# An attention stage in front of dense experts: squares without their scaling, sums of two operands, copies on ScalarE, an earlier weight load

## The chip, the cores and the metric

The kernel runs on one core of a Trainium2 chip. The metric is the device time of one execution in microseconds, the median of several runs. All arithmetic is fp32 (matmul operands are split into a high and a low part of a shorter form, so that three matmuls make one precise product).

## The reference

Three stages follow one another. The first is attention by random features over q, k, v of shape (2, 8, 576, 64) with 128 features:

```python
q_s, k_s = q * scale, k * scale               # scale = 64 ** -0.25
def phi(x):
    proj = x @ omega.T
    h = proj - sum(x * x) / 2                 # sum over the 64 of a head
    return exp(h - max(h)) / sqrt(128)
kv = phi(k_s).T @ v ; z = sum(phi(k_s))       # per batch and head
out = phi(q_s) @ kv / (phi(q_s) @ z + 1e-6)
```

Its output, seen as 1152 tokens of 512, goes through four experts (`relu(x @ w1[e]) @ w2[e]`, weighted by `p[:, e]` and summed) and then through `h = x @ w_in; (h * cos(h)) @ w_out`.

## The kernel before

Every engine's instructions are issued in an order written out by hand, in one program; engines run their own lists in order and wait for one another by semaphores. Attention is a loop of steps `s` over eight pairs of a batch and two heads, and a ninth for the 64 tokens of each head that are left over. Step `s` makes the features of q of pair `s` and of k of pair `s + 1`, finishes `kv` of pair `s - 1` and the numerators, and writes the output of pair `s - 2` into the token tile `x` (`put_x`: transposes `tx` on TensorE, high part `xh` on ScalarE, low part `xl` on VectorE). What comes ahead of step 0 (k and q of pair 0, k of pair 1, the left-over tokens of k) is written out in line.

The parts that the change touches:

- `norms_ahead` squares a tile of q or k on POOL and halves it by additions, 512 to 256 to 128 elements per partition, then scales it by `-SC * SC / 2` (line 1024). `features` reduces what is left on VectorE to one number per row (`three[:, :, 1]`, line 1074), takes the maxima of the projections `pj` from PSUM (`three[:, :, 0]`, line 1080), and makes of both the shift `nb` by two reductions over pairs of neighbours (lines 1089 and 1092). ScalarE's exponentials (`phk`, `phq`, line 1099) read `nb`. POOL's tiles of q and k are loaded by SP, two buffers each; a load waits until POOL and TensorE have read the buffer's old content.
- `k_features(s + 1, s < first)` puts off k's shift while `s` is under 6: it comes in the next step, behind VectorE's copy of `xT` (`turn_ahead`: q and k transposed, half copied by VectorE at line 1303, half by ScalarE at line 1301).
- `kv_of` copies the finished `kv` from PSUM on VectorE (line 1168).
- `load_a(0, p, "p")` and `load_v2` bring the first expert's weights: SP loads a piece `ra_0p`, `ra_1p`, ... into one of two `raw` buffers, ScalarE writes its high part (`w02h`, line 129), POOL the low part (`w02l`, `w1l`, ..., line 134). These are generators; `advance(wload)` moves each one on by one stage, twice in a step, and `fetched` says at the end of which step each begins. Piece 0 is loaded at the end of step 2, its high half made in the middle of step 4, its low half at the end of step 4.
- `dense` is the stream of the experts' matmuls. From step 6 on, some of them are placed in each attention step (`plain`, line 549, four quanta of six matmuls), and the first second-layer products (`g`, line 779) follow. Those read `sth` (ScalarE) and `stl` (VectorE, line 752).
- `token_sums` makes the sums of token columns (T1 to T4) that the first expert's blocks need, on VectorE and ScalarE, one stage per quantum of the stream. `less` (lines 300 to 303) makes two full-width subtractions.

Of the kernel before, what the change touches and what calls it, by code (L numbers as in the profile page):

```python
# [12 lines left out]
ACTF = mybir.ActivationFunctionType  # L13
ALU = mybir.AluOpType
AX = mybir.AxisListType
# [11 lines left out]
def performer_moe_kernel(ctx, tc, q, k, v, omega, probs, w1, w2, w_in, w_out, out):  # L27
    nc = tc.nc
# [16 lines left out]
    SC = float(D) ** -0.25  # L45
# [72 lines left out]
    LEAD = 5  # L118

    def wait(n):  # L120
        for _ in range(n):
            yield
# [31 lines left out]
    def load_a(e, p, what="as"):  # L154
        aside = (e, p) == (0, NPF - 1) and what == "as"
        if aside:
            raw = late["h"][:, :, p, :KD, :].rearrange("p i k f -> p i (k f)")
            r4 = late["h"][:, :, p, :KD, :]
        else:
            raw = new_raw(f"ra{e}_{p}{what}")  # L160
            r4 = raw.rearrange("p (i k f) -> p i k f", i=2, k=KD)
        if e < E:
            for i in range(2):
                f0 = (i * NPF + p) * P
                nc.sync.dma_start(
                    out=r4[:, i], in_=w1[e, :, f0 : f0 + P].rearrange("(k p) f -> p k f", p=P)
                )
        else:
            nc.sync.dma_start(out=raw, in_=kept["a", e, p][0])
        def shaped(parts):  # L170
            return [x.rearrange("p (i w) -> p i w", i=2) for x in parts] if aside else parts

        eng = nc.gpsimd if e == 0 and what != "as" else nc.vector
        yield from wait((3 if p < 3 else 2) if what == "p" else LEAD)
        if what != "s":
            kind = "p" if what == "p" else "a"
            yield from place(kind, e, p)
            parts = split(eng, raw, *shaped(units[kind, e, p]))
            next(parts)
            if (what, p) != ("p", 2):  # L180
                yield
            yield from parts
            loaded.add((kind, e, p))
        if what == "p":
            if p < 2:
                units["a", e, p] = units["p", e, p]
                holder[f"w{2 * p}"] = ("a", e, p)
                loaded.add(("a", e, p))
            return
        a11, a12, a21, a22 = (r4[:, i, 2 * j : 2 * j + 2] for i in range(2) for j in range(2))  # L190

        def op(dst, x, y, o):
            eng.tensor_tensor(out=dst, in0=x, in1=y, op=o)

        op(a22, a21, a22, ALU.add)
        op(a21, a11, a21, ALU.subtract)
        yield
        op(a11, a22, a11, ALU.subtract)
        op(a12, a12, a11, ALU.subtract)
        yield from wait(2 if e < E else int(e > E or p != 2))  # L200
        yield from place("s", e, p)
        more = split(eng, raw, *shaped(units["s", e, p]))
        next(more)
        yield
        yield from more
        loaded.add(("s", e, p))
# [92 lines left out]
    def less(r, n, ks, cols):  # L299
        h, l = (x.bitcast(F32) for x in tokens(n, ks, cols))  # L300
        minus(r, h, r)
        nc.vector.tensor_tensor(out=r, in0=r, in1=l, op=ALU.add)
# [35 lines left out]
    def token_sums(cols):  # L338

        r1, r2 = spare(cols)  # L340
        whole(r2, tokens(0, LO, cols))
        whole(r1, tokens(1, LO, cols))
        if not cols.start:
            yield
        minus(r1, r1, r2)
        yield
        parts = sum_out(1, r1, cols)
        next(parts)
        yield
        yield from parts  # L350
        less(r1, 1, HI, cols)
        yield
        yield from rest_sums(r1, r2, cols)
# [596 lines left out]
    with tc.tile_pool(name="at1", bufs=1) as at1, tc.tile_pool(name="at2", bufs=2) as at2:  # L950
# [63 lines left out]
        def norms_ahead(nm, t):  # L1014

            x2 = at2.tile([P, 2 * R, D], F32, tag=f"x2{nm[0]}", name=f"x2_{nm}")
            nc.gpsimd.tensor_tensor(out=x2, in0=t, in1=t, op=ALU.mult)
            w = D
            while w > 16:
                w //= 2  # L1020
                nc.gpsimd.tensor_tensor(
                    out=x2[:, :, 0:w], in0=x2[:, :, 0:w], in1=x2[:, :, w : 2 * w], op=ALU.add
                )
            nc.gpsimd.tensor_scalar(
                out=x2[:, :, 0:w], in0=x2[:, :, 0:w], scalar1=-SC * SC / 2, scalar2=None, op0=ALU.mult
            )
            sqs[nm] = x2[:, :, 0:w]

        def turn(nm, t, pieces=1):
# [28 lines left out]
        def features(nm, turned, phi, squares=None, shift_later=False):  # L1058

            nb = at2.tile([P, 2 * R], F32, tag=f"nb{nm}"[:3], name=f"nb_{nm}")  # L1060
            pjs = [bank(f"pj_{nm}_{g}") for g in range(2)]
            for i in range(R):
                c = slice(i * P, (i + 1) * P)
                for z, (x_, y) in enumerate([(turned, ws)] + [(squares, minus_norm)] * (squares is not None)):
                    for g, pj in enumerate(pjs):
                        r = slice(g * D, (g + 1) * D)
                        nc.tensor.matmul(
                            pj[:, i * M : (i + 1) * M], x_[r, c], y[r, :],
                            start=z == 0, stop=z == (squares is not None),
                        )  # L1070
            yield
            three = at2.tile([P, 2 * R, 3], F32, tag=f"th{nm[0]}", name=f"three_{nm}")
            def square_sum():
                nc.vector.tensor_reduce(out=three[:, :, 1], in_=sqs.pop(nm), op=ALU.add, axis=AX.X)

            if squares is None and nm != "q0":
                square_sum()
            for g, pj in enumerate(pjs):
                to = (nb if squares is not None else three[:, :, 0])[:, g : 2 * R : 2]
                nc.vector.tensor_reduce(  # L1080
                    out=to, in_=pj.rearrange("p (a m) -> p a m", m=M), op=ALU.max, axis=AX.X,
                    negate=squares is not None,
                )
            if shift_later:
                yield
            if squares is None:
                if nm == "q0":
                    square_sum()
                nc.vector.tensor_reduce(
                    out=three[:, :, 2], in_=three[:, :, 0:2], op=ALU.add, axis=AX.X, negate=True  # L1090
                )
                nc.vector.tensor_reduce(out=nb, in_=three[:, :, 1:3], op=ALU.add, axis=AX.X)
            yield
            order = [g + 2 * i for g in range(2) for i in range(R)]
            if squares is not None:
                order.insert(1, order.pop(R))
            for ix in order:
                i, g = divmod(ix, 2)
                nc.scalar.activation(  # L1099
                    phi[:, ix, :], pjs[g][:, i * M : (i + 1) * M], ACTF.Exp, bias=nb[:, ix : ix + 1]  # L1100
                )
# [38 lines left out]
        NPR = len(pairs)  # L1140
        xss, phks, phqs, kts, qts = {}, {}, {}, {}, {}

        kv = [at1.tile([P, 2, B, D + 1], F32, name=f"kv{hp}") for hp in range(NP)]
# [11 lines left out]
        def kv_of(i):  # L1155
            b, hp = pairs[i]
            ve, phk = ves[i % 2], phks.pop(i)
            kvp = room.pop() if room else bank(f"kv_{i}")
            kvp = kvp[:, 4 * (D + 1) : 6 * (D + 1)].rearrange("p (h e) -> p h e", h=2)
            for h in range(2):  # L1160
                for r in range(R):
                    column_halves(kvp[:, h, :], phk[:, h * R + r, :], ve[:, h * R + r, :], h == r == 0, False)
            yield
            for h in range(2):
                n = 2 * hp + h
                column_halves(kvp[:, h, :], phiL[:, n, :], veL[:, n, b, :], False, h == 1)
            yield
            nc.vector.tensor_copy(out=kv[hp][:, :, b, :], in_=kvp)

        pTs = {}  # L1170
        room = []
# [77 lines left out]
        for b in range(B):  # L1249
            nc.sync.dma_start(  # L1250
                out=pr[:, b * R : (b + 1) * R, :],
# [7 lines left out]
        first = 6  # L1259
        budget = [0.0]  # L1260
        wload = []
        fetched = {2: [("p", 0)], 3: [("p", 1)], 4: [("p", 2)], 5: [("p", 3), ("v", 0)]}
        fetched.update({6: [("v", 1), ("v", 2)], 7: [("v", 3)]})

        def dense_quanta(s, n):
# [41 lines left out]
        def k_features(s, shift_later=False):  # L1307
            phks[s] = at2.tile([P, 2 * R, M], F32, tag="phk", name=f"phk_{s}")
            return features(f"k{s}", turned.pop(("k", s)), phks[s], shift_later=shift_later)
# [46 lines left out]
        for s in range(NPR + 3):  # L1356
# [4 lines left out]
            else:  # L1361
# [29 lines left out]
                    b, hp = pairs[s - 2]  # L1391
                    px = put_x(f"{s - 2}", hp, xss.pop(s - 2), b * R, R)
                qs = q_features(s) if s <= NPR else iter(())
                ks = k_features(s + 1, s < first) if s + 1 < NPR else iter(())
                next(qs, None)
                next(ks, None)
                next(px, None)
# [78 lines left out]
```

## Time and profile before

| | |
|---|---|
| median of 3 runs | 640.66 us (640.45 to 641.06) |
| profiled execution | 640.92 us, of which span 639.1 us |
| busy in the span: TensorE matmuls | 632.7 us (99%) |
| VectorE | 488.7 us (76%) |
| ScalarE | 353.3 us (55%) |
| POOL | 174.4 us (27%) |
| granted TensorE clock | full, 0.999 of 1 |

The shares are means over unlike stages. Attention takes about the first 90 us. A matmul's busy time covers its way through a pipeline, so that many short ones in a row look like a full engine. An engine that idles costs nothing where another one sets the pace.

### The profile page before, as it was taken

To read this page: it belongs to the slowest core of one execution; us is meant where nothing else is said; L and a number is where in the kernel's file an instruction comes from. 1 tells how busy PE (TensorE), PEld (TensorE's weight loads), DVE (VectorE), ACT (ScalarE), POOL (GpSimd) and SP (SyncE) were. 2 spreads that over 40 slices of the span, in tenths; PEclk is the share of its full clock that TensorE was granted. 3 is DMA by queue.
4 is the path that set the end of the run, shared out by engine and by line. 5 is a ranking of instruction groups with operands and counts; after the bars stand their busy time and mean duration, and the time that the engine had idled before them with its cause. 6 is when DMAs were issued, how large, how long until landed. Compare 5 with 4: busy or idle time off the path is not lost.

```text
span 639.1 us, 10296 instructions
## 1 busy us (share of the span) xinstructions
PE 632.7 (99%) x3871; PEld 536.3 (84%) x3871; DVE 488.7 (76%) x877; ACT 353.3 (55%) x686; POOL 174.4 (27%) x217
## 2 busy tenths in 40 slices
PE   9999999999999999999999999999999999999997
PEld 8889988988888888888888888888888888888887
DVE  6998588789688688598687697699698772687842
ACT  6898664365346454354443455544457973476821
POOL 7899752033332333323333232310000000000000
PEclk9999999999999999999999999999999999999999
DMA  7644431313446433446334435301250002500111
GB/s 184 169 123 144 134 99 32 101 67 132 132 148 206 141 113 135 133 141 220 133 99 132 143 125 211 131 34 67 94 202 34 2 0 96 234 2 2 49 50 49
DMA packets 55442, 70.97 MB, mean 111 GB/s; under 512 B 15201, under 2 KB 40033, under 8 KB 55393
## 3 DMA queue, kind: packets, MB, share of 16 engines
q1 hardware_dynamic: 46800, 40.92, 20.3%
q0 software_dynamic: 8448, 29.37, 13.2%
q8 instruction: 30, 0.49, 0.3%
q14 instruction: 20, 0.16, 0.1%
q10 hardware_dynamic: 144, 0.03, 0.0%
HBM read 55.36 MB, written 14.94 MB: 110 GB/s over the span
## 4 chain that ended last, share of the span: by engine, by line
PE 86%; ACT 4%; DVE 4%; POOL 3%; issue 1%; DMA 1%; DVEq 0%; ACTq 0%; POOLq 0%
PE g L779 44%; PE g_odd L585 4%; PE g_1c L549 2%; PE g_0a L549 2%; PE g_3a L549 2%; PE g_2a L549 2%; PE g_1a L549 2%; PE g_2c L549 2%; PE g_3c L549 2%; PE g_0c L549 2%; ACT phk L1099 1%; PE g_0d L549 1%; PE g_0b L549 1%; PE g_3e L549 1%; PE g_3b L549 1%
## 5 line engine op out<-in xcount | busy, mean ns | idle before, releaser
L749 ACT ACTIVATE sth<-h 128x512 fp32r<-128x512 f32 (+1 forms) x111 | 60.3, 554 | 80.1 <-PE g L779 67.2
L258 POOL TENSOR_TENSOR c<-c 128x512 uint32<-128x512 uint32 x32 | 47.2, 1475 | 86.8 <-issue 34.0
L752 DVE SCALAR_TENSOR_TENSOR stl<-h,sth 128x512 fp32r<-128x512 f32 (+1 forms) x72 | 49.1, 697 | 26.7 <-ACT sth L749 26.6
L779 PE MATMUL g<-v2h,stl 128*128 128x512 f32 (+1 forms) x110 | 42.5, 386 | 0.6 <-DVE stl L752 0.6
L779 PE MATMUL g<-v3h,sth 128*128 128x512 f32 (+1 forms) x110 | 42.9, 390 | 0.0
L779 PE MATMUL g<-v0h,sth 128*128 128x512 f32 (+1 forms) x110 | 42.7, 388 | 0.0
L779 PE MATMUL g<-v1h,sth 128*128 128x512 f32 (+1 forms) x110 | 42.7, 388 | 0.0
L779 PE MATMUL g<-v2h,sth 128*128 128x512 f32 (+1 forms) x110 | 42.5, 386 | 0.0
L779 PE MATMUL g<-v0h,stl 128*128 128x512 f32 (+1 forms) x110 | 42.5, 386 | 0.0
L779 PE MATMUL g<-v3h,stl 128*128 128x512 f32 (+1 forms) x110 | 42.4, 386 | 0.0
L779 PE MATMUL g<-v1h,stl 128*128 128x512 f32 (+1 forms) x110 | 42.4, 386 | 0.0
L779 PE MATMUL g<-v1l,sth 128*128 128x512 f32 (+1 forms) x110 | 42.4, 385 | 0.0
L779 PE MATMUL g<-v0l,sth 128*128 128x512 f32 (+1 forms) x110 | 42.4, 385 | 0.0
L779 PE MATMUL g<-v3l,sth 128*128 128x512 f32 (+1 forms) x110 | 42.4, 385 | 0.0
L779 PE MATMUL g<-v2l,sth 128*128 128x512 f32 (+1 forms) x110 | 42.4, 385 | 0.0
L293 DVE TENSOR_TENSOR stl<-h,sth 128x512 fp32r<-128x512 f32 (+1 forms) x39 | 22.8, 593 | 19.3 <-ACT sth L749 19.1
L451 DVE SCALAR_TENSOR_TENSOR c<-c 128x512 f32<-128x512 f32 (+1 forms) x38 | 25.0, 662 | 11.9 <-ACT c L449 11.8
L448 ACT ACTIVATE c<-h 128x512 f32<-128x512 f32 x32 | 19.9, 622 | 19.9 <-DVE h L626 19.9
L805 DVE SCALAR_TENSOR_TENSOR acc<-g,pn,acc 128x512 f32<-128x512 f32 x27 | 20.1, 744 | 6.5 <-PE g L779 6.5
L779 PEld LDWEIGHTS g<-v2h,stl 128*128 128x128 f32 x110 | 20.7, 188 | 5.1 <-DVE stl L752 1.0
L779 PEld LDWEIGHTS g<-v0h,stl 128*128 128x128 f32 x110 | 20.7, 188 | 4.4 <-DVE stl L752 0.3
L779 PEld LDWEIGHTS g<-v3h,stl 128*128 128x128 f32 x110 | 20.7, 188 | 4.2
(437 smaller groups left out, 1877.3 us busy)
## 6 DMA issues: line engine op xcount, KB each, us to landing
rv<-in_moe_w_dram SPq DMA_DIRECT2D x16, 512.0 KB, 4.0
c<-in_moe_w_in_dram POOLq DMA_DIRECT2D x16, 512.0 KB, 4.1
c<-in_moe_w_out_dram POOLq DMA_DIRECT2D x16, 512.0 KB, 3.9
kt<-in_k_dram SPq DMA_DIRECT2D x8, 256.0 KB, 3.7
qt<-in_q_dram SPq DMA_DIRECT2D x8, 256.0 KB, 4.0
ve<-in_v_dram SPq DMA_DIRECT2D x16, 128.0 KB, 4.2
ra_2as<-in_moe_w_dram SPq DMA_DIRECT2D x8, 256.0 KB, 3.3
out_dram<-acc SPq DMA_DIRECT2D x7, 256.0 KB, 2.3
```

The costliest lines, as they stand in the source:

```text
L258: nc.gpsimd.tensor_tensor(out=total, in0=t, in1=lw, op=ALU.add)
L293: nc.vector.tensor_tensor(out=dst, in0=x, in1=y, op=ALU.subtract)
L448: nc.scalar.activation(vv, src, ACTF.Copy, bias=0.25, scale=INV_2PI)
L451: nc.vector.scalar_tensor_tensor(out=vv, in0=kk, scalar=ROUND, in1=vv, op0=ALU.subtract, op1=ALU.subtract)
L549: nc.tensor.matmul(dst, x[:, o], y[:, kk], start=start and n == 0, stop=stop and n == 3 * kn - 1, skip_group_check=reopen,)
L585: nc.tensor.matmul(g, x[:, kk], w[:, :, :, kk, :], start=n == 0, stop=n == 3 * KD - 1)
L749: nc.scalar.activation(hi, src, ACTF.Relu if self.e < E else ACTF.Copy)
L752: nc.vector.scalar_tensor_tensor(out=to, in0=src, scalar=0.0, in1=hi.bitcast(F32), op0=ALU.max, op1=ALU.subtract)
L779: nc.tensor.matmul(g, x, y[:, o : o + w], start=n == 0, stop=n == 3 * FT - 1)
L805: nc.vector.scalar_tensor_tensor(out=acc[t], in0=src, scalar=p_, in1=acc[t], op0=ALU.mult, op1=ALU.add)
L1099: nc.scalar.activation(phi[:, ix, :], pjs[g][:, i * M : (i + 1) * M], ACTF.Exp, bias=nb[:, ix : ix + 1])
```

## The change

Five edits. POOL no longer scales the squares; VectorE makes the two sums of the shift by SCALAR_TENSOR_TENSOR, which multiplies the sum of squares by the constant and adds or subtracts a second operand. The shift of k follows its maxima at once in all steps. Three of the eight `kv` copies go to ScalarE, behind the exponentials of k. Piece 0 of the weights is loaded at the end of step 0 and its high half is made at the top of step 1; its low half stays at the end of step 4. The token sums of columns 1 to 4 yield once more ahead of `less`.

```diff
-        yield from wait((3 if p < 3 else 2) if what == "p" else LEAD)
+        yield from wait((1, 3, 3, 2)[p] if what == "p" else LEAD)
...
             next(parts)
-            if (what, p) != ("p", 2):
-                yield
+            yield from wait((7, 1, 0, 1)[p] if what == "p" else 1)
             yield from parts
...
         yield from parts
+        if cols.start:
+            yield
         less(r1, 1, HI, cols)
...
-            nc.gpsimd.tensor_scalar(
-                out=x2[:, :, 0:w], in0=x2[:, :, 0:w], scalar1=-SC * SC / 2, scalar2=None, op0=ALU.mult
-            )
...
-                nc.vector.tensor_reduce(
-                    out=three[:, :, 2], in_=three[:, :, 0:2], op=ALU.add, axis=AX.X, negate=True
-                )
-                nc.vector.tensor_reduce(out=nb, in_=three[:, :, 1:3], op=ALU.add, axis=AX.X)
+                for out, x, op in ((three[:, :, 2], three[:, :, 0], ALU.add), (nb, three[:, :, 2], ALU.subtract)):
+                    nc.vector.scalar_tensor_tensor(
+                        out=out, in0=three[:, :, 1], scalar=-SC * SC / 2, in1=x, op0=ALU.mult, op1=op
+                    )
...
-            nc.vector.tensor_copy(out=kv[hp][:, :, b, :], in_=kvp)
+            if i in (1, 2, 3):
+                nc.scalar.activation(kv[hp][:, :, b, :], kvp, ACTF.Copy)
+            else:
+                nc.vector.tensor_copy(out=kv[hp][:, :, b, :], in_=kvp)
...
-        fetched = {2: [("p", 0)], 3: [("p", 1)], 4: [("p", 2)], 5: [("p", 3), ("v", 0)]}
+        fetched = {0: [("p", 0)], 3: [("p", 1)], 4: [("p", 2)], 5: [("p", 3), ("v", 0)]}
...
-                ks = k_features(s + 1, s < first) if s + 1 < NPR else iter(())
+                ks = k_features(s + 1) if s + 1 < NPR else iter(())
```

## Rows read from the trace of the kernel before

**Rows 1.** Waits of TensorE in the first 150 us: total us, times, longest.

```profile
PE pj_k L1067 <- ACT phk L1099: 1.1, 4, 0.4
...
PE g L779 <- DVE stl L752: 0.6, 1, 0.6
```

**Rows 2.** Busy time in a stretch: TensorE, its loads, VectorE, ScalarE, POOL; clock, DMA.

```profile
30.00:40.00 10.00, 9.70 (x197) 8.71 (x198) 9.60 (x30) 9.60 (x32) 8.95 (x14) 1.00 0.73 209
```

**Rows 3.** Timeline of VectorE, steps 3 to 5: start, duration, line, operation.

```profile
28.02 0.68 DVE L1303 COPY xT<-tp 128x512 f32<-128x512 f32 x1
...
29.97 0.28 DVE L1168 COPY kv<-num 128x130 f32<-128x130 f32 x1
...
33.56 1.28 DVE L1080 TENSOR_REDUCE three_k<-pj_k 128x4 f32<-128x512 f32 x2
34.75 0.68 DVE L1303 COPY xT<-tp 128x512 f32<-128x512 f32 x1
...
41.73 0.69 DVE L1303 COPY xT<-tp 128x512 f32<-128x512 f32 x1
```

**Rows 4.** Timeline of TensorE (PEld: its weight loads), step 3.

```profile
30.21 0.52 PEld L1067 LDWEIGHTS pj_k<-ws,xT 64*128 64x128 f32 x8 [0.39 <-ACT phk L1099]
...
31.31 0.66 PE L1122 MATMUL tx<-ident,xs 128*128 128x128 f32 x4
```

**Rows 5.** Timeline of ScalarE, steps 1, 3 and 4.

```profile
19.23 2.18 ACT L1099 ACTIVATE phq<-pj_q,nb_q 128x128 f32<-128x128 f32 x8 [0.98 <-DVE nb_q L1092]
...
32.00 0.66 ACT L1134 ACTIVATE xh<-tx 128x384 fp32r<-128x384 f32 x2 [0.32 <-PE tx L1122]
...
35.24 1.12 ACT L129 ACTIVATE w02h<-ra_0p 128x1024 fp32r<-128x1024 f32 x1
```

**Rows 6.** Groups by line and shape, first 92 us: busy us, mean ns | idle before.

```profile
L1017 POOL TENSOR_TENSOR x_k<-kt 128x512 f32<-128x512 f32 x8 | 8.3, 1040 | 2.9 <-DMA kt<-in_k_dram 2.3
...
L1021 POOL TENSOR_TENSOR x_k<-x_k 128x256 f32<-128x256 f32 x8 | 5.8, 728 | 0.6
...
L1024 POOL TENSOR_SCALAR x_k<-x_k 128x128 f32<-128x128 f32 x8 | 4.2, 530 | 0.7
...
L1021 POOL TENSOR_TENSOR x_k<-x_k 128x128 f32<-128x128 f32 x8 | 3.6, 454 | 0.6
```

**Rows 7.** Timeline of VectorE and POOL in step 6 and from 87 us.

```profile
54.73 1.28 DVE L1080 TENSOR_REDUCE three_k<-pj_k 128x4 f32<-128x512 f32 x2
54.99 2.53 POOL L134 TENSOR_TENSOR w1l<-ra_2p,w1h 128x512 fp32r<-128x512 f32 x2
56.04 0.17 DVE L1089 TENSOR_REDUCE three_k<-three_k 128x8 f32<-128x16 f32 x1
...
56.33 0.20 DVE L1433 RECIPROCAL psum__161<-psum__161 128x9 f32<-128x9 f32 x1
56.57 1.00 DVE L1434 TENSOR_TENSOR pn<-pr,psum__161 128x36 f32<-128x36 f32 x1
...
87.54 3.37 POOL L193 TENSOR_TENSOR ra_1s<-ra_1s 128x256 f32<-128x256 f32 x4 [1.20 <-DMA ra_1s<-in_moe_w_dram]
87.61 2.70 DVE L752 SCALAR_TENSOR_TENSOR stl<-c,sth 128x256 fp32r<-128x256 f32 x3
```

**Rows 8.** Timeline of VectorE ahead of the first expert's blocks.

```profile
98.49 0.42 DVE L752 SCALAR_TENSOR_TENSOR stl<-c,sth 128x256 fp32r<-128x256 f32 x1
```

**Rows 9.** Timeline of SP's queue at step 0: start and length of issues.

```profile
14.02 1.26 SPq L996 DMA_DIRECT2D ve<-in_v_dram  x2
17.23 0.37 SPq L987 DMA_DIRECT2D kt<-in_k_dram  x1
```

**Rows 10.** Loads of weight pieces: KB each, median us from issue to landing.

```profile
ra_0p<-in_moe_w_dram SPq DMA_DIRECT2D x2, 256.0 KB, 3.9
ra_1p<-in_moe_w_dram SPq DMA_DIRECT2D x2, 256.0 KB, 4.0
...
ra_3p<-in_moe_w_dram SPq DMA_DIRECT2D x2, 256.0 KB, 2.8
```

## The prediction

> **What bounds the kernel now.** I read the waits of TensorE first, then busy time by stretch, then the timelines of one attention step, and last the landings of the loads. In the first 150 us TensorE waits in three places. One is the warm-up. One is `pj_k`, four times, 1.1 us in all. The third is 0.6 us for `stl`, just before the first expert's blocks [rows 1]. Behind that it waits for no other engine, so a time that these 99 us gain or lose is the kernel's. From 30 to 40 us VectorE is busy 9.60 of 10, ScalarE as much and POOL 8.95, while TensorE runs many short matmuls whose busy time overstates it [rows 2]. In steps 2 to 5 a ring of three engines sets the pace, and in step 3 it can be followed. VectorE copies `xT` at 28.02, TensorE projects q and then k (`pj_k` at 30.21) and transposes `tx` at 31.31, ScalarE copies `xh` at 32.00, VectorE subtracts `xl`, reduces `three_k` from 33.56, and copies the next `xT` at 34.75: 6.73 us [rows 3 to 5]. From step 6, when the dense matmuls enter, TensorE has no gap. The chain of waits leads through POOL in steps 6 and 7, but that is the order of releases, no wait of TensorE.
>
> **The change part by part.** Sums are made against the profiled execution, 640.92 us (span 639.1 and 1.8 around it), 0.26 above the median of the three runs, 640.66.
>
> *Scaling of squares.* 17 instructions of 0.53 us leave POOL, 9.0 us [rows 6] (the nine for q are like the eight for k). Nobody on the ring waits for POOL, so alone this is worth nothing. Its other effect is that a norm now has three POOL instructions, of 1.04, 0.73 and 0.45 us, all reading SBUF, 2.22 us in place of 2.75.
>
> *The two reductions become SCALAR_TENSOR_TENSOR.* If nothing holds them they cost what the reductions do, 0.17 us each [rows 7], and the part is worth 0. But the old ones read one operand and the new ones read two, both in SBUF. At 56.04, inside POOL's `w1l` (54.99 for 2.53), the reduction takes 0.17. At 56.57 VectorE adds 36 elements from two SBUF operands under the same POOL work, and takes 1.00 us: it ends at 57.57, when `w1l` has ended at 57.52. At 87.61 three subtractions of 256 elements take 2.70 us beside four POOL instructions of 3.37 [rows 7]; at 98.49, with POOL idle, one takes 0.42 [rows 8]. So each waited for about one POOL instruction, and behind each of them the next POOL instruction came in first. The trace has no such instruction of 8 elements. Its price lies between 0 (POOL idle) and, per pair, 1.04 for the first and 1.04 for the second. I take an estimate from these rows. Arriving at random in a norm, the first waits (1.04² + 0.73² + 0.45²) / (2 × 2.22) = 0.41, the second, which needs the first one's result, a whole next instruction, mean 0.74: 1.15 while POOL is busy. In steps 1 to 5 POOL has ten norms and two low halves (10 × 2.22 + 2 × 2.5 = 27.2 us) in five steps of about 8 us, a share of 0.68: 0.78 a pair.
>
> The rows show this for an add and a subtraction. The Trainium skill (SBUF — State Buffer, "Who interferes with whom") states it generally: a VectorE instruction with two SBUF inputs and a GpSimd instruction that reads SBUF share a read interface, the first to start keeps it to its end, and a reduction on this chip is never in the contest. By that rule the old pair was exempt and the new one isn't, whatever its size. By the 0.17 us rows alone this part would be worth 0, by the rule the same 7 us as below.
>
> How many are on the path: k's five pairs (k2 to k6) lie in the ring, 5 × 0.78 = 3.9. q's five (q1 to q5) stand on VectorE before `xl`, which has some 0.25 us of air once the `kv` copy is gone, so 5 × 0.53 = 2.65. In the lead-in k0 and k1 delay ScalarE's exponentials by 1.6, of which 1.1 are covered by the load below: 0.5. The pairs of steps 6 to 8 have TensorE's queue of dense matmuls as cover and cost nothing. Sum +7.0; bounds 0 and, each held twice for 1.04, some 14.
>
> *Shift of k earlier.* Before, `nb_k` came behind the copy of `xT`; ScalarE's exponentials started late, and the weights of `pj_k` waited 0.39 in step 3 for the bank that these read [rows 4]. Without that wait the ring would be 6.34. Now the dependent pair stands in the ring. Step 6 already has this order: from its `three_k` at 54.73 to the instruction behind the pair, at 56.33, pass 1.60 [rows 7], against 1.19 from 33.56 to 34.75 [rows 3], 0.41 more. 6.34 + 0.41 = 6.75 against 6.73: nothing in steps 2 to 5, and in step 6 a `pj_k` earlier by 0.2 to 0.4. I take -0.2; bounds -0.4 and +0.4.
>
> *Three `kv` copies to ScalarE.* VectorE loses 0.28 us [rows 3], ScalarE gains as much. It falls where ScalarE waits 0.32 for `tx` [rows 5]; that wait hides it. 0; without that cover 3 × 0.28 = +0.8.
>
> *First weight piece.* Its high half (1.12 us) leaves step 4, where the ring took 6.98 (34.75 to 41.73 [rows 3]) in place of 6.73: -0.25. It goes to the top of step 1, ahead of the exponentials `phq` of q1, where ScalarE is idle for 0.98 us up to 19.23 [rows 5]. The copy fits if its load has landed by 18.25. SP ends the last issue before it at 15.28 [rows 9]; the piece has two DMAs, the second some 0.6 later, and such a pair took 3.9 to 4.0 us from issue to landing behind the same loads, 2.8 in a quiet queue [rows 10]: between 18.7 and 19.9. The exponentials then start between 19.7 and 20.9, 0.5 to 1.7 late, and behind them on ScalarE stand `xT` and `phk`, for which TensorE's `pj_q` waits; the ring has no air to take that back. I take 1.1, so this part is +0.85 (bounds +0.2, +1.45). SP's next load started only at 17.23, so its two issues delay no load behind them. The low half stays where it was on POOL.
>
> *Token sums.* `less`, two subtractions over the whole tile, now comes after the two `stl` that TensorE waits for [rows 8]; VectorE's work in front of T2 and later is the same, only in another order, so their tiles are ready as before. -0.6; bounds -0.7 and 0, if TensorE meets T3's low half 0.6 us sooner and waits there.
>
> Sum: 0 + 7.0 - 0.2 + 0 + 0.85 - 0.6 = +7.05. That is 648.0 for a profiled execution, 647.7 for the median; as a hold under way also lets POOL finish its norms sooner against a longer step, I put it a little lower, 647.5.
>
> **The rivals.** (1) *Nothing is held.* POOL, freed of 9 us, has its norms done when the pairs come, or so short an instruction slips between. Then the sum is +0.05, 640.7, no change. For it: POOL's norms are bound by their loads once they are shorter. Against it: POOL was busy 8.95 of 10 us, and a pair comes once the loads of its step have landed. It decides if fewer than one pair in six waits. (2) *The load lands in ScalarE's hole*, by 18.25, with nothing held: the +1.1 goes, and the sum is -1.05, 639.6, at best 639.3 with the bounds of the shift and the token sums. For it: the hole is there; against it: 2.8 us is the shortest landing of such a pair, and gives 18.7. (3) *POOL is the path from 49 to 68 us*, as the chain of waits says. Then five scalings there shorten it by 5 × 0.53 = 2.65, and with -0.6 for the token sums the kernel takes 637.4. For it: POOL has no gap there; against it: TensorE's list of waits names no POOL. (4) *The load lands at 20 us or later* and the kernel is slower by that alone, 0.6 over rival 1: 641.3, still no change. For it: the queue is full then; against it: two such pairs landed in 3.9 to 4.0.
>
> **How the numbers follow.** A measurement of this kernel tells some 0.2% (1.3 us) from no change. Forecast 0.77; rival 1 0.11, rival 2 0.04, rival 3 0.04, rival 4 0.04. The forecast's own range is 644 to 651 (the 7.0 and half of it less or more). Faster by over 0.2%: rival 3 and half of rival 2, with a little of rival 1's edge: 0.07. Within: rival 1, the rest of 2, most of 4, and a bottom of the forecast, 0.15. Slower: 0.78. To hold eight in ten the range reaches to rival 1: 640.2 to 650.5.
>
> **What would show it.** Right: SCALAR_TENSOR_TENSOR rows on `three` and `nb` with a mean of some 0.5 us against 0.17, the longest about 1 us and ending with POOL instructions; steps of 7.5 to 8.5 us; the first dense matmuls some 7 us later; ScalarE waiting for `ra_0p` near 18.3; no `stl` wait of TensorE before the blocks. Wrong: those rows at 0.2 us or less with POOL busy; dense matmuls less than 2 us later; a new wait of TensorE for T2 or T3 behind the blocks' start; POOL so far ahead that it idles whenever a pair comes.

## The result, and the profile after

The changed kernel takes 644.44 us (median of 6 runs, 643.46 to 646.32) against 640.87 for the kernel before (6 runs, 640.45 to 641.06). The medians lie 3.6 us apart, where 6.8 were forecast. The ratio, made from all runs, is 1.0061, with a 95% interval of 1.0044 to 1.0078, which is 3.9 us. The direction and the main mechanism came out; the size is about half, and not every term of the sum stood.

The profiled execution took 646.32 (span 644.5); it and the run of 645.95 show a mean granted clock of TensorE of 0.997 and the other four, 643.46 to 644.47, one of 0.999 or 1.0, so some 2 us of what the following rows show in steps 1 and 2 aren't in the median.

The first view is the list of TensorE's waits in the changed kernel, where [rows 1] named `pj_k` and `stl`.

```profile
PE pj_q L1065 <- DVE rd L1108: 2.9, 4, 1.1
PE tq L1146 <- ACT phq L1097: 1.2, 3, 0.8
PE tq L1146 <- DVE rd L1108: 1.2, 1, 1.2
...
PE g_0c L550 <- DVE h L627: 0.3, 1, 0.3
```

TensorE now waits mostly for VectorE (`rd` opens the chain that frees the bank of `num` for `pj_q`) and for ScalarE's exponentials. The wait for `stl` is gone, and a new one, for `h`, stands in the first expert's blocks. The row of busy time that answers to [rows 2] says who sets the pace:

```profile
30.00:40.00 10.00, 8.69 (x199) 7.74 (x197) 9.82 (x26) 8.11 (x28) 6.15 (x8) 1.00 0.47 134
```

VectorE is busy 9.82 us of 10, POOL only 6.15. The timelines of VectorE and POOL around one of k's pairs show what VectorE spends its time on:

```profile
30.07 0.28 DVE L1072 TENSOR_REDUCE three_k<-x_k 128x8 f32<-128x128 f32 x1
30.26 1.28 DVE L1078 TENSOR_REDUCE three_k<-pj_k 128x4 f32<-128x512 f32 x2
31.58 0.72 DVE L1088 SCALAR_TENSOR_TENSOR three_k<-three_k 128x8 f32<-128x8 f32 x1
32.33 0.17 DVE L1088 SCALAR_TENSOR_TENSOR nb_k<-three_k 128x8 f32<-128x8 f32 x1
...
32.62 0.68 DVE L1304 COPY xT<-tp 128x512 f32<-128x512 f32 x1
...
40.25 0.68 DVE L1304 COPY xT<-tp 128x512 f32<-128x512 f32 x1
```

```profile
30.43 1.04 POOL L1018 TENSOR_TENSOR x_k<-kt 128x512 f32<-128x512 f32 x1 [0.82 <-DVE three_k L1072]
31.55 1.28 POOL L1022 TENSOR_TENSOR x_k<-x_k 128x256 f32<-128x256 f32 x2
```

The first of the pair starts 0.03 us after POOL's first addition and ends with it (31.55 + 0.73 against 31.58 + 0.72). Such a row, which takes longer than 0.17 us and ends when POOL's instruction does, is called held below. The second starts in the gap between POOL's two additions and takes 0.17. From this copy of `xT` to the next pass 7.63 us; before it was 6.73 and 6.98 [rows 3]. Grouped by line and shape over the first 92 us, the pairs' 34 instructions take 13.7 us (mean 0.40), where 34 reductions of 0.17 were 5.8:

```profile
L1088 DVE SCALAR_TENSOR_TENSOR nb_q<-three_q 128x8 f32<-128x8 f32 x9 | 4.2, 462 | 0.3
L1088 DVE SCALAR_TENSOR_TENSOR three_k<-three_k 128x8 f32<-128x8 f32 x8 | 4.0, 497 | 0.3
L1088 DVE SCALAR_TENSOR_TENSOR three_q<-three_q 128x8 f32<-128x8 f32 x9 | 3.9, 434 | 0.3
...
L1088 DVE SCALAR_TENSOR_TENSOR nb_k<-three_k 128x8 f32<-128x8 f32 x8 | 1.6, 201 | 0.4
```

The other change is on ScalarE in step 1, where [rows 5] had a hole of 0.98 us before `phq`:

```profile
20.96 1.06 ACT L129 ACTIVATE w02h<-ra_0p 128x1024 fp32r<-128x1024 f32 x1 [2.26 <-DMA ra_0p<-in_moe_w_dram]
21.93 2.16 ACT L1097 ACTIVATE phq<-pj_q,nb_q 128x128 f32<-128x128 f32 x8
```

ScalarE waits 2.26 us for the piece's landing at 20.96, and the exponentials of q1 start at 21.93 where they started at 19.23. The first dense matmul starts at 58.21, 5.8 us later than before (52.37); in e2 below, whose profiled execution had the full clock, it starts at 55.99.

### The profile page after: what moved, and what is told of

Same layout as the page of the kernel before. It is cut to its first block, busy times and chain, and to the rows that moved or that the text cites. A ratio compares the mean times of both kernels' runs of the same rounds, so it can differ in the third digit from the quotient of the medians.

```text
span 644.5 us, 10279 instructions
## 1 busy us (share of the span) xinstructions
PE 633.6 (98%) x3871; PEld 537.6 (83%) x3871; DVE 494.1 (77%) x874; ACT 353.8 (55%) x689; POOL 165.1 (26%) x200
## 4 chain that ended last, share of the span: by engine, by line
PE 93%; DVE 4%; ACT 2%; issue 0%; DVEq 0%
PE g L780 46%; PE g_odd L586 4%; PE g L550 3%; PE g_1c L550 2%; PE g_0c L550 2%; PE g_2a L550 2%; PE g_3a L550 2%; PE g_1a L550 2%; PE g_3c L550 2%; PE g_2c L550 2%; PE g_0a L550 2%; PE g_0d L550 1%; PE g_0b L550 1%; PE g_0e L550 1%; PE g_3e L550 1%; PE g_3b L550 1%
## 5 line engine op out<-in xcount | busy, mean ns | idle before, releaser
L449 ACT ACTIVATE c<-h 128x512 f32<-128x512 f32 x32 | 19.9, 621 | 19.9 <-DVE h L627 19.9
L780 PEld LDWEIGHTS g<-v1h,stl 128*128 128x128 f32 x110 | 20.7, 188 | 4.2
```

The costliest lines, as they stand in the source:

```text
L449: nc.scalar.activation(vv, src, ACTF.Copy, bias=0.25, scale=INV_2PI)
L780: nc.tensor.matmul(g, x, y[:, o : o + w], start=n == 0, stop=n == 3 * FT - 1)
```

## The experiments

Twelve kernels, each timed in five rounds beside the kernel before (medians of 640.69 to 641.13 there). The first four undo one part of the change, or make one alone. The edits are shortened: `...` stands for code left out, and `<-` for an instruction's output and input.

**e1, reductions back.**

```
-  (no scaling)      for out, x, op in (...): nc.vector.scalar_tensor_tensor(...)
+  nc.gpsimd.tensor_scalar(out=x2.., scalar1=-SC * SC / 2, op0=ALU.mult)
+  nc.vector.tensor_reduce(three[:, :, 2] <- three[:, :, 0:2], negate=True)
+  nc.vector.tensor_reduce(nb <- three[:, :, 1:3])
```

> The changed kernel with POOL's scaling and VectorE's two reductions as before; all else stays changed. Before is 640.9 us, after 644.4. Theory (held pairs and ScalarE's wait for the piece both cost): the pairs' share goes, some 0.55 us for each pair held in the ring, and what is left is the wait for the piece, 2.5 us, less 0.25 in step 4, 0.6 for the token sums and 0.2 for the shift: 642.3, between 641.5 and 643. Rival A (the piece alone cost it, holds are absorbed): 644 or more, no change against after. Rival B (the held pairs alone cost it): 640.3, as before less the token sums.

Measured: 642.54, ratio 1.0028 (1.0017 to 1.0039). This is the theory's number; both rivals are out.

**e2, piece back.**

```
-  yield from wait((1, 3, 3, 2)[p] ...      fetched = {0: [("p", 0)], 3: ...
-  yield from wait((7, 1, 0, 1)[p] ...
+  yield from wait((3 if p < 3 else 2) ...  fetched = {2: [("p", 0)], 3: ...
+  if (what, p) != ("p", 2): yield
```

> The changed kernel with the first weight piece loaded and split as before; all else stays changed. Theory (both cost): the pairs held for 0.55 us in steps 1 to 5, four of k and some of q's three, give 2 to 3 us, less 0.8 for the token sums and the shift: 642.5, between 641.8 and 643.5. Rival A (the piece alone): 640.2. Rival B (the pairs alone): 644.

Measured: 644.33, ratio 1.0058 (1.0046 to 1.0070). Here rival B gave the number: without the early piece the kernel is as slow as with it. With e1 this means that the parts don't add up.

**e3, pair alone**, in the kernel before: the reverse of e1's edit.

> The kernel before with one part of the change: POOL's scaling gone and the pair of SCALAR_TENSOR_TENSORs in place of the two reductions. Theory (both cost): the pairs are held, 0.17 us become some 0.7 in one of each pair, and the kernel takes 642 to 644. Rival A (the piece alone): 640.9, or a little less if POOL's shorter norms bring something.

Measured: 643.13, ratio 1.0045 (1.0028 to 1.0062), as the theory has it.

**e4, piece alone**, in the kernel before: the reverse of e2's edit.

> The kernel before with one part of the change: the first weight piece loaded in step 0 and its high half made in step 1. Theory (both cost): ScalarE waits some 2 us for the landing, 2.5 us of it reach the end and 0.25 come back in step 4: 643, between 642 and 644; TensorE's clock falls for some us where it waits longest. Rival B (the pairs alone): 640.8.

Measured: 641.86, ratio 1.0021 (1.0010 to 1.0031), between theory and rival. The twelve runs are of two kinds: seven with a mean granted clock of 0.999 or 1.0 took 640.6 to 642.0 (median 641.54), five with 0.997 took 642.78 to 644.5 (median 643.19). The profiled one is of the first kind; in it ScalarE waits 1.48 us for the piece where e1's waits 3.18, so the wait differs with the landing.

**e11, both back**: the changed kernel with the edits of e1 and e2; the shift's order, the `kv` copies and the token sums stay.

> The changed kernel with the piece and the scaling with its two reductions both as before; the shift's order, the three kv copies on ScalarE and the token sums stay changed. Theory (the small parts are worth what the prediction says, and the pairs cost all that e2 lost): 640.9 less 0.6 for the token sums and 0.2 for the shift, 640.1. Rival C (the new order of shift and copies costs by itself, because TensorE's pj_q now waits for a bank that VectorE frees later): 641.5 to 642.5.

Measured: 640.81, ratio 0.9999 (0.9991 to 1.0008). The three small parts together are worth nothing, neither the 0.8 us of the theory nor the loss of rival C. Where the 0.6 us of the token sums went is in this kernel's timelines of VectorE and TensorE:

```profile
97.07 0.42 DVE L754 SCALAR_TENSOR_TENSOR stl<-acc,sth 128x256 fp32r<-128x256 f32 x1
97.40 0.95 DVE L293 TENSOR_TENSOR h<-xh,h 128x768 f32<-128x768 f32 x1
...
104.12 0.96 DVE L134 TENSOR_TENSOR T4l<-h,T4h 128x768 fp32r<-128x768 f32 x1
105.69 0.56 DVE L628 TENSOR_TENSOR h<-g_0d,h 128x384 f32<-128x384 f32 x1 [0.62 <-ACT h L634]
```

```profile
107.63 0.44 PE L551 MATMUL g_0c<-T4h,w02h 128*128 128x384 f32 x1 [0.25 <-DVE h L628]
```

VectorE's work from `stl` to T4's low half at 104.12 is the same as before, only in another order. TensorE reaches the blocks at 100.73 in place of 101.36, finds at 107.63 that VectorE has not yet freed the bank for `g_0c`, and goes on there at the time at which the kernel before did.

**e6, no scaling, piece back**: e11 without POOL's scaling.

```
-  nc.gpsimd.tensor_scalar(out=x2.., scalar1=-SC * SC / 2, op0=ALU.mult)
```

> As e11, but nobody scales the squares: POOL is as free as in the changed kernel and VectorE keeps the two reductions of one input. It leaves out the factor on the squares. Theory (what costs is the second SBUF input of the pair): 640.1, as e11, and the reductions take 0.17 us beside the same POOL instructions that hold the pair for 0.72. Rival D (POOL's faster pace, locked to VectorE's, costs, whatever the pair's form): 642 or more.

Measured: 640.30, ratio 0.9992 (0.9983 to 1.0001), as the theory has it: POOL has as little to do as in the changed kernel, the reductions read one input, and nothing is lost. Of all runs this one and e2 are the closest pair: they differ in the form of VectorE's two instructions alone (and in the factor, which only e2's form applies), and lie 644.33 - 640.30 = 4.0 us apart. A reduction of VectorE and the POOL instruction under which it runs, here:

```profile
31.59 0.17 DVE L1088 TENSOR_REDUCE three_q<-three_q 128x8 f32<-128x16 f32 x1
31.80 0.17 DVE L1091 TENSOR_REDUCE nb_q<-three_q 128x8 f32<-128x16 f32 x1
```

```profile
31.24 1.04 POOL L1019 TENSOR_TENSOR x_q<-qt 128x512 f32<-128x512 f32 x1
```

Both reductions lie whole inside POOL's 1.04 us and take 0.17 each.

**e10, scaling on VectorE, piece back**: the reductions, and one more VectorE instruction ahead of them.

```
+  nc.vector.tensor_scalar(out=three[:, :, 1], in0=three[:, :, 1], scalar1=-SC * SC / 2, op0=ALU.mult)
```

> As e6, with the scaling put on VectorE as one more instruction of one input ahead of the two reductions. Theory (from step 1 to 5 VectorE sets the pace, so what a pair takes longer counts in full): 0.2 us for each of some ten pairs, 642.1, between 641.3 and 642.6. Rival E (only k's five pairs lie in the ring, as the prediction has it, with q's half covered): 1 to 1.5, 641.3.

Measured: 643.72, ratio 1.0045 (1.0033 to 1.0058). More than either number, since the new instruction is held as well, with only one SBUF input. VectorE and POOL at one of q's:

```profile
41.13 1.05 DVE L1088 TENSOR_SCALAR three_q<-three_q 128x8 f32<-128x8 f32 x1
42.22 0.17 DVE L1091 TENSOR_REDUCE three_q<-three_q 128x8 f32<-128x16 f32 x1
```

```profile
41.11 1.04 POOL L1019 TENSOR_TENSOR x_q<-qt 128x512 f32<-128x512 f32 x1
```

It starts 0.02 us after POOL's multiplication and takes 1.05, where those that meet no POOL instruction, or only its end, take 0.16 to 0.18; the reductions behind it take 0.17. So this run doesn't measure 0.2 us a pair, as it was meant to, and says nothing on rival E. It shows that being held is a matter of the operation and not only of the number of inputs.

**e5, copy later**: the changed kernel, with the piece loaded in step 0 and its high half made just ahead of step 4's copy of `xT` on ScalarE.

```
-  wait((1, 3, 3, 2)[p] ...   wait((7, 1, 0, 1)[p] ...
+  wait((6, 3, 3, 2)[p] ...   wait((2, 1, 0, 1)[p] ...
```

> The changed kernel with the piece still loaded in step 0, but its high half made some steps later; POOL's low half stays where it was. Theory (the piece costs by ScalarE's wait for its landing, in order ahead of the exponentials): the wait of 2.3 us goes, the pairs stay held: 643.5, between 642.5 and 644.5. Rival F (the early load's traffic and its delay of the q and v loads cost): 644.4 or more, as the changed kernel, with TensorE or POOL waiting for q or v.

Measured: 643.83, ratio 1.0044 (1.0030 to 1.0057). In the theory's range, but too near to 644.4 to tell the two apart.

**e12, late copy with the reductions**: the edits of e1 and e5 together.

> As e1 (642.5: scaling and reductions as before, the piece loaded in step 0), with the piece's high half made in step 4 as before and not in step 1. Theory (ScalarE's wait for the landing, with the exponentials behind it, is all that the early load costs): as e11, 640.8, between 640.3 and 641.2. Rival F (the load's traffic and what it delays cost too): 641.5 to 642.5.

Measured: 640.78, ratio 1.0001 (0.9992 to 1.0010). This tells them apart: with the reductions the early load costs nothing, and what e1 lost was ScalarE's wait in front of its exponentials.

**e13, split addition**: e2, with POOL's first addition in four.

```
-  nc.gpsimd.tensor_tensor(out=x2[:, :, 0:w], ...)
+  for r in range(0, 2 * R, 2 if w == 32 else 2 * R):
+      nc.gpsimd.tensor_tensor(out=x2[:, z, 0:w], ...)
```

> As e2 (644.3), with POOL's first addition of a norm, 0.73 us, cut into four. Theory (a pair waits for the end of the one POOL instruction that it meets, most often this addition): the held row falls from 0.72 us to 0.2 to 0.45, and the kernel to between 642 and 643.5. Rival G (VectorE waits until POOL has no reading work in line, however it is cut): the held rows stay at 0.7 or grow, and the kernel stays at 644.3 or more.

Measured: 644.78, ratio 1.0062 (1.0048 to 1.0076). The time is the rival's, the rows are the theory's. Of VectorE, a pair that met a cut addition, and later one that met the low half of a weight piece:

```profile
34.93 0.43 DVE L1091 SCALAR_TENSOR_TENSOR three_q<-three_q 128x8 f32<-128x8 f32 x1
35.40 0.17 DVE L1091 SCALAR_TENSOR_TENSOR nb_q<-three_q 128x8 f32<-128x8 f32 x1
...
49.27 0.45 DVE L1091 SCALAR_TENSOR_TENSOR three_q<-three_q 128x8 f32<-128x8 f32 x1
49.75 1.21 DVE L1091 SCALAR_TENSOR_TENSOR nb_q<-three_q 128x8 f32<-128x8 f32 x1
```

```profile
34.30 1.04 POOL L1019 TENSOR_TENSOR x_q<-qt 128x512 f32<-128x512 f32 x1
35.41 1.72 POOL L1025 TENSOR_TENSOR x_q<-x_q 128x64 f32<-128x64 f32 x5
...
48.41 2.51 POOL L134 TENSOR_TENSOR w02l<-ra_1p,w02h 128x512 fp32r<-128x512 f32 x2
```

The pairs from 27 to 46 us take at most 0.50 an instruction, none 0.72, and the three steps from 24.21 to 45.29 take 6.94, 7.13 and 7.01, against 7.50, 7.64 and 7.49 in e2. But the low half that POOL makes at 48.41 holds q5's pair for 0.45 and 1.21 (in e2 that pair met nothing), and ahead of step 1 two rows of the pairs take 0.96 that take 0.17 in e2, with the first copy of `xT` at 14.34 for 13.29. What the cut gained in three steps was lost in the others. The profiled execution, 646.29, is the longest of the five, with a mean clock of 0.997 against 0.999 in e2's.

**e7, sums alone**, in the kernel before.

```
+  if cols.start:
+      yield
   less(r1, 1, HI, cols)
```

> The kernel before with one part of the change: the token sums of a later range yield once more, so that the two stl come ahead of less. The prediction gave this part 0.6 us: 640.3. Theory now (VectorE has no gap from 94 to 105 us, so what TensorE gains at the stl it loses some 6 us later, at the bank of g_0c that VectorE frees): 640.9, no change, with a wait of 0.2 to 0.6 us for h behind the blocks' start.

Measured: 640.34, ratio 0.9998 (0.9989 to 1.0007): no change. The wait for `stl` is gone from TensorE's list, and in its place stands the one that e11 shows (TensorE goes on there at 107.40 for 107.63, which the runs can't tell from no gain):

```profile
PE g_0c L551 <- DVE h L628: 0.3, 1, 0.3
```

**e15, shift as before**: e2, with k's pair behind the copy of `xT`.

```
-  ks = k_features(s + 1) ...
+  ks = k_features(s + 1, s < first) ...
```

> As e2 (644.3), with k's pair behind the copy of xT again in steps 0 to 5; the kv copies and the token sums stay changed. e3, which has this order too, took 643.1. Theory (ahead of the copy, a held pair delays the copy and with it TensorE; behind it, part of its hold is covered): 643.1, between 642.5 and 643.7. Rival H (VectorE has no air in these steps, so a hold costs the same on either side of the copy, and e2 and e3 differ by chance or by the kv copies): 644.0 or more.

Measured: 642.90, ratio 1.0041 (1.0025 to 1.0057), the theory's number, and that of e3, which shares this order. The intervals of e2 and e15 overlap a little; among the runs with a clock of 0.999 or 1.0 they don't (four of e15 from 642.48 to 642.94, five of e2 from 643.72 up). The theory's cause of these 1.4 us need not be the only one: in e15's profiled execution k's pairs of steps 1 to 5 are also held for less, 1.1 us in all against 2.7 in e2: behind the copy of `xT` the pair comes later, and meets only the end of POOL's addition (0.30 at 29.67 and 0.25 at 36.67, where e2 has 0.73 twice). No run separates a shorter hold from one that is better covered.

## Why the prediction was right, and where it was off

*What holds the pairs: right.* Undoing the pairs alone gives back some 2 us of 3.6 (e1), making them alone costs 2.2 (e3), and held rows end with POOL instructions. It is the pair's form and not POOL's new pace: e2 and e6 differ in the form alone, 4.0 us apart, and e6 loses nothing. The Trainium skill (SBUF — State Buffer, "Who interferes with whom") states that two SBUF inputs contend with a POOL instruction that reads SBUF, that a reduction never contends on this chip, and that a `tensor_scalar` can, in a mode that takes both ports. These runs agree on the first two (0.72 beside an addition of 0.73; 0.17 inside 1.04) and show a `tensor_scalar` held (1.05 beside 1.04), but not in which mode it was.

*Its price: mis-sized.* The prediction gave the pairs +7.0; e2 against e11, which differ in the pairs and POOL's scaling, says 644.33 - 640.81 = 3.5, and against e6, which has no scaling either, 4.0. The step that failed is 0.78 a pair: an arrival at random in a norm, and for the second "a whole next instruction". Neither holds. The rows of the ten pairs in steps 1 to 5 of the profiled execution are 4.2 us above 0.17 each, 0.42 a pair; in e2's they are the same. The second starts where POOL's instruction has just ended, and POOL's next comes only 0.08 later, so it slips in: behind the five firsts that were held in steps 2 to 4 (0.72 to 0.75 us), the second took 0.17 every time. Two pairs went otherwise: k2's second started 0.11 after its first had ended and was held as well (0.74 and 0.42), and of q4's it was the second alone (0.72). What the first meets is not drawn at random either. With shorter norms and longer steps POOL has caught up, and in four of the five it waits for VectorE's reduction of the previous squares to free their tile (0.82 at 30.43). It starts its 1.04 us multiplication then, VectorE its two `pj` reductions of 1.28, and both come out together: the pair meets the 0.73 us addition at its very start. It isn't the longest of POOL's instructions, and in step 5, where POOL had nothing left to do, neither pair met anything.

*Which pairs count: the ring had changed.* The prediction put k's pair in the ring and gave q's 0.25 us of air. VectorE at 9.82 of 10 us has no air, so a step loses what both its pairs lose: 7.63 − 6.73 = 0.9, near 0.55 for k plus 0.55 for q less the 0.28 of the `kv` copy. The 0.5 of the lead-in isn't shown: there k0 and q0 are held for 0.6 in all, and the first copy of `xT` came at 13.27 for 12.77, but in runs that have the reductions there it comes anywhere from 12.22 (e11) to 13.40 (e4).

*Shift of k earlier: wrong in sign, with the pairs held.* With the reductions it is worth nothing (e11). With held pairs it costs some 1.4 us (e2 against e15), since k's pair then meets POOL's addition from its start, or since the copy of `xT`, and with it TensorE, waits behind the hold; which of the two counts for more stays open. The prediction worked out -0.2 from undisturbed rows, beyond whose +0.4 this lies; it is part of the 3.5 above.

*First weight piece: right in kind, uncertain in size.* Alone it costs 0.9 us (e4), and 1.7 beside the reductions and the new order (e1 against e11). That 0.9 is near the +0.85 is luck: it is the median over runs of two kinds, which cost 0.6 (full clock) and 2.2 (0.997). e12 shows that ScalarE's wait is all of it. But the landing was later than the 18.7 to 19.9 given: 20.35 to 20.96 in e4 and the changed kernel, 4.8 us from issue to landing where [rows 10] had 2.8 to 4.0. It wasn't the new place that made it later: in the executions of e7 and e2, with the piece at its old place, it took 5.4 and 5.7, and in e12, at the new one, 4.4. The 3.9 of [rows 10] is the shortest of all fourteen profiled executions, and the prediction took that one execution for the rule. On top of the held pairs the piece costs next to nothing (644.44 against 644.33). In the changed kernel's trace a reason can be seen that no run isolates: POOL waits 1.90 us for a load of q, its norms shift, and q1's pair in step 1, which in e2 takes 0.70 and 0.17, takes 0.17 twice.

*Token sums: wrong.* The -0.6 is 0 within the runs' spread (e7, e11). The prediction saw that TensorE could come 0.6 us early to something and wait there, and put it in the bounds; it looked at T3's low half, and it was the bank of `g_0c`.

*Scaling removed, and `kv` copies: 0, as said.* With the reductions the scaling's removal changes nothing clear of the spread (e6 against e11), and the copies, the shift and the token sums are 0 together (e11). Whether POOL's freed time does harm beside held pairs, by the meeting point above, isn't shown: no run keeps the scaling with the new pair. Of the rivals, 1 and 2 (nothing held) fall by the held rows, and 3 by e6, which frees POOL and gains at most the 1.1 us of its interval. Of rival 4 the late landing came true, but not that nothing else costs (e3).

As measured, then, the sum is 3.5 for the pairs and the shift, next to nothing for the piece on top of them, and 0 for the rest. That is 3.6, at the low end of the forecast's own 644 to 651; that it isn't below owes something to luck, since the token sums gave back nothing of their 0.6.

Open: how much of the piece's price is chance of the landing and of the clock, and whether the piece really buys back holds in step 1. No run here beats the kernel before; e6 might by a little, but it leaves out a factor.

## What to carry to other kernels

Where VectorE sets the pace beside a busy POOL, the form of even an instruction of 8 elements a partition decided its price: here a reduction of one tile was not held, while two SBUF inputs or a `tensor_scalar` were, for up to the length of one POOL instruction. Saving an instruction on an engine that nobody waits for brought nothing (e6). What an instruction meets can follow from who releases whom, and then an estimate by random arrival is off. And an early transfer helps nobody if its consumer stands in order on a full engine before the landing; a wait removed is only a gain once the next shared engine has been looked at.

## What was not expected of the hardware

A `TENSOR_SCALAR` of 128x8 elements with one SBUF input took 1.05 us beside a POOL instruction of 1.04, and 0.16 to 0.18 where it met none or only its end (e10).

In the profiled execution of the changed kernel TensorE's clock fell. The busy time by stretch of 2 us, whose last three columns are the granted clock, the share and the rate of DMA:

```profile
20.00:22.00 2.00, 1.92 (x56) 1.64 (x50) 1.86 (x4) 1.04 (x2) 1.84 (x3) 1.00 1.06 300
22.00:24.00 2.00, 0.27 (x1) 0.13 (x1) 1.99 (x8) 2.00 (x10) 1.70 (x3) 0.95 0.72 191
24.00:26.00 2.00, 1.86 (x24) 1.86 (x26) 0.81 (x2) 2.00 (x9) 1.84 (x4) 0.50 0.87 235
26.00:28.00 2.00, 2.00 (x26) 1.89 (x24) 1.08 (x3) 1.30 (x5) 1.92 (x3) 0.70 0.07 16
```

TensorE did one matmul in 2 us, while it waited for ScalarE and VectorE, and then ran its next 16 `pj_q` at 0.50 of full speed, the lower of its two levels, 1.2 GHz: they took 2.12 us for 1.16. In e1 the stall was longer, 1.05 and 0.27 us busy in the same two stretches, and the clock stayed at 1.00:

```profile
20.00:22.00 2.00, 1.05 (x26) 0.84 (x24) 1.86 (x9) 0.99 (x2) 1.76 (x4) 1.00 1.00 282
22.00:24.00 2.00, 0.27 (x1) 0.14 (x1) 0.83 (x4) 2.00 (x10) 1.84 (x3) 1.00 0.18 42
24.00:26.00 2.00, 1.81 (x35) 1.76 (x37) 1.02 (x3) 2.00 (x9) 1.75 (x4) 1.00 0.63 183
```

So a wait of 2 us ahead of TensorE may cost about that much again, or not, from run to run. Nor does the clock fall behind such a wait alone: in e13's profiled execution it stood at 0.57 over 54 to 58 us, and in the 8 us ahead, where TensorE was busy 7.18, no wait was longer than 0.44. A mean clock of 0.997 is on record for 17 runs, all of kernels with the new pair or with the piece's high half in step 1, and for none of the kernel before or of e6, e7, e10, e11 and e12; the spread of the changed kernel, 2.9 us against 0.6 before, comes from it in the main.
